# Score visits across batch borders, one mask on GpSimd and an earlier weight load in an attention + squared-ReLU kernel

## The chip, the cores and the metric

The kernel runs on one core of one Trainium2 chip. The metric is the device time of one execution in microseconds (us). Ratios are the mean time of one kernel's fast runs over that of the other kernel's fast runs of the same rounds, so they are not quite the ratio of the medians quoted beside them. The rounds of the experiments ran on three chips of the same kind, each with before measured in the same rounds, so ratios compare better than medians of different rounds.

## The reference

Attention with 16 "beacon" keys per head in front of the causal keys, then a feed-forward layer with squared ReLU, over all tokens. Cut to what matters:

```python
B, H, S, Nb, D = 8, 8, 576, 16, 64           # q, k, v: (B, H, S, D); beacon_k, beacon_v: (B, H, Nb, D)
scores = q @ concat(beacon_k, k).T / sqrt(D)  # causal for k, open for the 16 beacon keys
a = softmax(scores)
x = (a @ concat(beacon_v, v)) as (B*S, H*D)   # 4608 x 512
h = relu(x @ w_in)                            # w_in 512 x 2048
out = (h * h) @ w_out                         # w_out 2048 x 512
```

## The kernel before

The kernel is a list of small operations, each with a priority, dependencies and a guessed duration. A list scheduler in Python walks them once and so fixes the order of instructions on each engine; on the chip each engine then runs its own list in order and waits for semaphores. The order is thus a result of the guesses, but the times are the chip's. The attention of batches 1 to 7 is woven into the feed-forward work (first layer: `w_in`; second layer: `w_out`) of nine chunks of 512 tokens.

Three parts matter. First, the score matmuls of batches 1 to 7. A batch has 13 pieces of 512 columns (two heads each); TensorE does them in "visits" of two or three pieces, between other work:

```python
    PLAN = ((2,2,3,3,3),(2,2,3,3,3),(2,3,3,3,2),(2,3,3,3,2),(2,3,3,3,2),(2,3,3,3,2),(2,3,3,3,2))
    # ... in add_batch(b):
        for size in PLAN[b - 1]:
            pos = HP * b + 512.0 * n / PW
            runs = [(0,), (1, 2)] if size == 3 else [tuple(range(size))]
            # ... one PE op per run; a triple's first piece goes to two single PSUM banks, the rest to strips
            n += size
        assert n == NPC      # every batch ends with a visit of its own
```

Second, the triangle masks of batch 0 (a minimum with a triangle on VectorE; zeroing with an affine select on GpSimd), of which one is on GpSimd:

```python
        on_pool = n == 1 and p in (2, )
        mask = add(f"mask{p}.{n}", "POOL" if on_pool else "DVE", ...)
```

Third, the order of GpSimd's work in the start, where it issues nearly all loads and does some casts. `p1k` is a load of q or k, `v0` a load of v, `w0` a quarter of `w_in`, `c2` the cast of the third v load, `m2` the mask of pair 2:

```python
    SOFT = "t0 p1k p1q t1 p2k p2q v0 v1 p3k p3q v2 v3 v4 w0 w1 c2 c3 c4 w2 w3 m2".split()
    # then: batch 1's k and q, its v, and the four quarters of w_out
    w_ops["out", i] = add(f"wout{i}", "POOL", 1.3, emit, ..., dma=2.6)
```

The softmax here doesn't subtract the row's maximum and nothing guards it: scores larger than these inputs give would overflow.

## Time and profile before

| | before |
|---|---|
| time, median of the first three runs (and of 11 in later rounds) | 338.1 us (338.0) |
| span of the profiled execution | 336.9 us |
| TensorE matmul busy | 97% |
| VectorE, ScalarE, GpSimd busy | 51%, 56%, 28% |
| last quarter of w_out lands | 50.49 us |
| last matmuls of attention start (only feed-forward work after) | 263.3 us |

"Busy" is the share of the span with an instruction in flight. TensorE at 97% does not mean that it is at its peak: what can be read from the trace is when each matmul starts. The prediction below shows the lines.

### The profile page before, as it was taken

What the parts mean: (1) busy time and instruction counts of PE and PEld (TensorE: products, weight loads), DVE (VectorE), ACT (ScalarE), POOL (GpSimd) and SP (SyncE); (2) the same over time, 40 slices, a digit from 0 to 9 for tenths busy, and PEclk for the clock granted to TensorE, in tenths of its full rate; (3) what the DMA queues carried; (4) which work ended last, traced back from release to release, by engine and by line L of the source; (5) the groups of instructions that cost most, each with busy time, mean ns of one, the idle gap of its engine ahead of it and who ended that gap; (6) DMA issues with size and microseconds to landing.
All of it is one profiled execution on the core that took longest, in us unless ns stands there. A gap on an engine that the chain in (4) does not pass through costs nothing.

```text
span 336.9 us, 7807 instructions
## 1 busy us (share of the span) xinstructions
PE 328.4 (97%) x3153; PEld 188.0 (56%) x3196; DVE 170.6 (51%) x393; ACT 189.6 (56%) x287; POOL 93.3 (28%) x146
## 2 busy tenths in 40 slices
PE   8999999999999999999999999999999999999996
PEld 6587866444564554545458845554555544444444
DVE  4896986048646983477145723674247302301400
ACT  3875874277468735476647674666557216515621
POOL 9694714226305513250334142404000000000000
PEclk9999999999999999999999999999999999999999
DMA  7999999999999997999899999998210221011003
GB/s 138 216 193 217 205 182 205 230 243 214 173 230 221 193 199 141 222 235 186 150 213 215 166 196 163 219 229 159 74 62 2 46 90 62 0 61 66 1 2 125
DMA packets 143955, 51.74 MB, mean 154 GB/s; under 512 B 130702, under 2 KB 138798, under 8 KB 143918
## 3 DMA queue, kind: packets, MB, share of 16 engines
q1 hardware_dynamic: 135375, 42.19, 63.4%
q0 software_dynamic: 7904, 8.69, 15.3%
q8 instruction: 25, 0.41, 0.5%
q10 hardware_dynamic: 639, 0.36, 0.4%
q14 instruction: 12, 0.10, 0.1%
HBM read 37.22 MB, written 9.44 MB: 138 GB/s over the span
## 4 chain that ended last, share of the span: by engine, by line
PE 83%; DMA 10%; POOL 5%; issue 1%; ACT 0%; POOLq 0%; ACTq 0%
PE ps L955 35%; PE ps L917 33%; PE ps L754 8%; PE strip L624 4%; DMA w_out<-in_moe_w_out_dram 4%; DMA qk_area<-in_q_dram 3%; DMA stg<-in_v_dram 2%; PE ps L624 2%; POOL qk_area L452 2%; PE ps L867 1%; POOL stg L372 1%; PE ps L821 1%; POOL w_out L854 0%; POOL w_in L846 0%; POOL vb L328 0%
## 5 line engine op out<-in xcount | busy, mean ns | idle before, releaser
L917 PE MATMUL ps<-xT,w_in 128*128 128x512 bf16 (+3 forms) x686 | 131.4, 339 | 0.7
L955 PE MATMUL ps<-w_out,g 128*128 128x512 bf16 x535 | 127.1, 379 | 2.1 <-DMA w_out<-in_moe_w_out_dram 0.5
L917 PEld LDWEIGHTS <-w_in 128*128 128x128 bf16 x704 | 65.6, 98 | 51.0 <-issue 0.7
L933 ACT ACTIVATE g<-ps 128x512 bf16<-128x512 f32 (+2 forms) x113 | 64.0, 566 | 45.8 <-PE ps L917 42.7
L633 ACT ACTIVATE pt<-strip 128x1024 bf16<-128x1024 f32 (+3 forms) x86 | 81.2, 1003 | 13.1 <-PE strip L624 13.0
L942 DVE TENSOR_TENSOR g<-g 128x1024 bf16<-128x1024 bf16 (+2 forms) x80 | 51.1, 648 | 66.9 <-ACT g L933 65.4
L955 PEld LDWEIGHTS <-g 128*128 128x128 bf16 x560 | 51.5, 98 | 57.4 <-issue 2.1
L328 POOL CAST qk_area<-stg 128x512 bf16<-128x512 f32 (+2 forms) x60 | 40.9, 689 | 62.9 <-DMA stg<-in_k_dram 39.3
L326 ACT COPY osb<-ps 128x512 f32<-128x512 f32 (+2 forms) x32 | 18.1, 570 | 58.6 <-PE ps L955 48.8
L328 POOL CAST vb<-stg 128x512 bf16<-128x512 f32 (+1 forms) x38 | 25.2, 670 | 70.6 <-DMA stg<-in_v_dram 70.3
L754 PEld LDWEIGHTS <-pt 128*128 128x128 bf16 (+1 forms) x960 | 36.4, 98 | 11.8 <-issue 0.9
L754 PE MATMUL ps<-vb,pt 128*128 128x65 bf16 (+1 forms) x960 | 39.5, 194 | 0.1
L726 DVE TENSOR_TENSOR pt<-pt,tri 128x512 bf16<-128x512 bf16 x63 | 29.6, 478 | 17.6 <-ACT pt L675 10.9
L935 DVE TENSOR_SCALAR g<-ps 128x512 bf16<-128x512 f32 (+2 forms) x47 | 27.4, 598 | 13.1 <-PE ps L917 12.6
L773 DVE TENSOR_TENSOR xn<-ps,rcp 128x320 bf16<-128x320 f32 (+2 forms) x64 | 31.5, 492 | 2.5 <-DVE rcp L771 0.2
L675 ACT ACTIVATE pt<-ps 128x512 bf16<-128x512 f32 x42 | 22.8, 597 | 15.9 <-PE ps L624 13.3
L771 DVE RECIPROCAL rcp<-ps 128x5 f32<-128x5 f32 (+2 forms) x64 | 12.2, 190 | 32.1 <-PE ps L754 31.4
L624 PEld LDWEIGHTS <-kT 64*128 64x128 bf16 x596 | 19.8, 94 | 15.3 <-issue 13.6
L624 PE MATMUL strip<-qT,kT 64*128 64x208 bf16 (+13 forms) x474 | 27.0, 239 | 0.0
L328 DVE COPY osb<-ps 128x512 f32<-128x512 f32 (+1 forms) x6 | 3.8, 625 | 20.8 <-PE ps L867 11.7
L296 PE MATMUL ps<-g 128*128 128x128 bf16 (+1 forms) x82 | 9.7, 271 | 1.1 <-DVE warm L303 1.1
L372 POOL DMA_DIRECT2D stg<-in_v_dram x10 | 8.6, 875 | 4.0 <-DMA w_in<-in_moe_w_in_dram 2.8
(45 smaller groups left out, 98.4 us busy)
## 6 DMA issues: line engine op xcount, KB each, us to landing
out_dram<-osb SPq DMA_DIRECT2D x17, 512.0 KB, 4.4
stg<-in_q_dram SPq DMA_DIRECT2D x24, 256.0 KB, 4.8
stg<-in_k_dram SPq DMA_DIRECT2D x18, 256.0 KB, 5.3
stg<-in_v_dram SPq DMA_DIRECT2D x18, 256.0 KB, 4.9
w_in<-in_moe_w_in_dram POOLq DMA_DIRECT2D x4, 512.0 KB, 9.0
w_out<-in_moe_w_out_dram POOLq DMA_DIRECT2D x4, 512.0 KB, 11.5
stg<-in_v_dram POOLq DMA_DIRECT2D x6, 256.0 KB, 8.5
stg<-in_k_dram SPq DMA_DIRECT2D x6, 224.0 KB, 4.1
```

The lines of the kernel that those rows point to most:

```text
L328: eng[e].tensor_copy(dst, src)
L624: nc.tensor.matmul(st[hj][:, at:at + t1 - t0], kT[b % 2][hp, pr, 128 * c:128 * c + 128], qT[b % 2][hp, pr, t0:t1], start=True, stop=True,)
L633: nc.scalar.activation(pt[:, :, at:at + width], strips[qk.slots[s]][:, :, 0:width], AF.Exp, bias=0.0, scale=scale)
L675: nc.scalar.activation(pt[:, hj, at:at + 512], ps[qk.wide[hj]], AF.Exp, bias=0.0, scale=scale)
L726: nc.vector.tensor_tensor(out=d, in0=d, in1=tri[:, m0:m0 + m, :][:, None].to_broadcast([128, 2, m, 128]), op=ALU.min)
L754: nc.tensor.matmul(a[:, at + (t - tl[0]) * (D + 1):at + (t - tl[0] + 1) * (D + 1)], P[0:rr, hj, o:o + 128], vb[b % 2][0:rr, c, 2 * pr + hj ...
L773: nc.vector.tensor_tensor(out=xn[b % 2].rearrange("p t (h d) -> p h t d", d=D)[:, h0:h0 + nh, tl[0]:tl[0] + nt], in0=a[:, :, :, 0:D], in1= ...
L917: nc.tensor.matmul(h[:, lo - spans[0][0]:hi - spans[0][0]], w_in_sb[:, mc, ft * 128:(ft + 1) * 128], xT[:, mc, lo % RING:lo % RING + hi - lo],
L933: nc.scalar.activation(dst, h, AF.Relu, bias=0.0, scale=1.0)
L935: nc.vector.tensor_scalar(out=dst, in0=h, scalar1=0.0, scalar2=None, op0=ALU.max)
L942: nc.vector.tensor_tensor(out=d, in0=d, in1=d, op=ALU.mult)
L955: nc.tensor.matmul(o, G[:, fc, ts * 128:(ts + 1) * 128], w_out_sb[:, fc, :], start=(fc == 0), stop=(fc == NFT - 1))
```

## The change

The intent: fewer, fuller score visits from batch 4 on, less work for VectorE in the crowded start, and the third quarter of `w_in` in the queue before GpSimd sits down to wait for v. Cut to its core (the score code is reorganised into a class so that a visit can hold pieces of two batches; its instructions are the same):

```diff
-    PLAN = ((2,2,3,3,3),(2,2,3,3,3),(2,3,3,3,2),(2,3,3,3,2),(2,3,3,3,2),(2,3,3,3,2),(2,3,3,3,2))
+    sizes = list((2,2,3,3,3, 2,2,3,3,3, 2,3,3,3,2, 3,3,3,3,3,3,3,3,3,3,3,3,3,3,3,3,2,2))
...
+        for n in range(NPC):
+            if not opened:
+                opened.append(Visit(b, n, sizes.pop(0)))
+            opened[0].add(b, n)
+            if len(opened[0].parts) == opened[0].size:
+                opened.clear()
...
-        on_pool = n == 1 and p in (2, )
+        on_pool = n == 1 and p in (1, 2, )
...
-    (transposes of batch 0's first part: prio ... - 500.0; their copies to xT on DVE only)
+    (the same: prio ... - 2500.0; their copies on ACT or DVE)
...
-    SOFT = "t0 p1k p1q t1 p2k p2q v0 v1 p3k p3q v2 v3 v4 w0 w1 c2 c3 c4 w2 w3 m2".split()
+    SOFT = "t0 p1k p1q t1 p2k p2q v0 v1 p3k p3q v2 v3 v4 w0 w1 w2 c2 c3 m1 c4 w3 m2".split()
```

More of the change, by code (lines that the diff above doesn't have):

```diff
@@ L639, with __init__, emit, banks @@
     SHIFT = 0.25
-    PLAN = ((2,2,3,3,3),(2,2,3,3,3),(2,3,3,3,2),(2,3,3,3,2),(2,3,3,3,2),(2,3,3,3,2),(2,3,3,3,2))
     FREE = 2
-    last_qk = []
+    sizes = list((2,2,3,3,3, 2,2,3,3,3, 2,3,3,3,2, 3,3,3,3,3,3,3,3,3,3,3,3,3,3,3,3,2,2))
+    assert sum(sizes) == NPC * (B - 1)
+    last_qk, opened = [], []
+    class Visit:
+        def __init__(self, b, n, size):
+            pos = HP * b + 512.0 * n / PW
+            self.size, self.parts, self.ops = size, [], []
+            for k, run in enumerate([(0,), (1, 2)] if size == 3 else [tuple(range(size))]):
+                def emit(e, run=run):
+                    for s in run:
+                        bb, m = self.parts[s]
+                        emit_scores(bb, PIECES[m], self.banks(s))
+                self.ops.append(add(
+                    f"qk{b}.{n + run[0]}", "PE", (0.1 if size == 3 else 0.2) + 512 * len(run) / 2400.0, emit,
+                    prio=-1.0e6 if k else 100.0 * pos - 1000.0,
+                    behind=self.ops[-1:] if k else last_qk[-1:] if size == 3 or b > FREE else [],
+                    take=None if k else ("strip", "strip", min(size, 2)), gate=None if k else gate_at(pos - SHIFT)))
+            self.ops[0].wide = [None] if size == 3 else []
+            last_qk.append(self.ops[-1])
+        def banks(self, s):
+            first = self.ops[0]
+            if self.size == 3 and s == 0:
+                return [ps[x] for x in first.wide]
+            st = strips[first.slots[s - (self.size == 3)]]
+            return [st[:, 0, :], st[:, 1, :]]
+        def add(self, b, n):
+            s = len(self.parts)
+            self.parts.append((b, n))
+            first, op = self.ops[0], self.ops[-1 if s else 0]
+            at, prio = 512 * n, 1.0e-2 * (HP * b + 512.0 * n / PW) - 30.0
+            if self.size == 3 and s == 0:
+                es = []
+                for hj in range(2):
+                    def emit_half(e, hj=hj):
+                        nc.scalar.activation(pt[:, hj, at:at + 512], ps[first.wide[hj]], AF.Exp, bias=0.0, scale=scale)
+                    es.append(add(f"exp{b}.{n}.{hj}", "ACT", 0.18 + 512 / 1200.0, emit_half, prio=prio + 1.0e-4 * hj,
+                                  deps=[op], give=(first, hj - 2)))
+            else:
+                es = [add_exp(f"exp{b}.{n}", first, s - (self.size == 3), at, 512, prio, op)]
+            for pr in sorted({mm[0] for mm in PIECES[n]}):
+                p = HP * b + pr
+                for o in deps_of(b, pr, 0) + av_ops[p - HP]:
+                    if o not in first.need:
+                        first.need.append(o)
+                qk_ops[p].append(op)
+                exps_of[p] += es
@@ L647, in add_batch @@
             qk_ops[p], av_ops[p], exps_of[p] = [], [], []
-        n = 0
-        for size in PLAN[b - 1]:
-            pos = HP * b + 512.0 * n / PW
-            box = {}
-            runs = [(0,), (1, 2)] if size == 3 else [tuple(range(size))]
-            for k, run in enumerate(runs):
-                def emit(e, run=run, n=n, box=box, size=size):
-                    for s in run:
-                        if size == 3 and s == 0:
-                            emit_scores(b, PIECES[n], [ps[x] for x in box["qk"].wide])
-                        else:
-                            st = strips[box["qk"].slots[s - (size == 3)]]
-                            emit_scores(b, PIECES[n + s], [st[:, 0, :], st[:, 1, :]])
-                qk = add(f"qk{b}.{n + run[0]}", "PE", 0.2 / len(runs) + 512 * len(run) / 2400.0, emit,
-                         prio=-1.0e6 if k else 100.0 * pos - 1000.0, behind=[qk] if k else last_qk[-1:] if size == 3 or b > FREE else [],
-                         take=None if k else ("strip", "strip", min(size, 2)), gate=None if k else gate_at(pos - SHIFT))
-                last_qk.append(qk)
-                if k == 0:
-                    qk.wide = [None] if size == 3 else []
-                    box["qk"] = qk
-                for s in run:
-                    at, prio = 512 * (n + s), 1.0e-2 * (pos + 0.1 * s) - 30.0
-                    if size == 3 and s == 0:
-                        es = []
-                        for hj in range(2):
-                            def emit_half(e, hj=hj, at=at, qk=qk):
-                                nc.scalar.activation(pt[:, hj, at:at + 512], ps[qk.wide[hj]], AF.Exp, bias=0.0, scale=scale)
-                            es.append(add(f"exp{b}.{n}.{hj}", "ACT", 0.18 + 512 / 1200.0, emit_half, prio=prio + 1.0e-4 * hj, deps=[qk],
-                                          give=(qk, hj - 2)))
-                    else:
-                        es = [add_exp(f"exp{b}.{n + s}", box["qk"], s - (size == 3), at, 512, prio, qk)]
-                    for pr in sorted({mm[0] for mm in PIECES[n + s]}):
-                        p = HP * b + pr
-                        for o in deps_of(b, pr, 0) + av_ops[p - HP]:
-                            if o not in box["qk"].need:
-                                box["qk"].need.append(o)
-                        qk_ops[p].append(qk)
-                        exps_of[p] += es
-            n += size
@@ L689, in add_batch @@
-        assert n == NPC
+        for n in range(NPC):
[4 more added lines that the diff above has]
+                opened.clear()
         for pr in range(HP):
@@ L822, in emit_tp @@
                                             xn[b % 2][0:n, t, 128 * pr:128 * pr + 128], ident[0:n, 0:n])
-                tp = add(f"xtp{b}.{k}.{pr}", "PE", 0.02 + 0.05 * len(ph.tiles) + (0.1 if b == 0 else 0.0), emit_tp, prio=-120.0 - (500.0 if b == 0 and len(ph.tiles) == 2 else 0.0),
+                tp = add(f"xtp{b}.{k}.{pr}", "PE", 0.02 + 0.05 * len(ph.tiles) + (0.1 if b == 0 else 0.0), emit_tp, prio=-120.0 - (2500.0 if b == 0 and len(ph.tiles) == 2 else 0.0),
                          deps=norm_ops[HP * b + pr, k], take=("ps", "tp"))
@@ L831, in emit_ev @@
                     copy_on(e, xT[:, pr, at + lo:at + hi], pp[:, lo:hi])
-                o = add(f"xte{b}.{k}.{pr}", ("ACT", "DVE") if b or k else ("DVE",),
-                        {"ACT": 0.2 + (hi - lo) / 1200.0, "DVE": 0.12 + (hi - lo) / 960.0}, emit_ev, prio=-110.0 - (500.0 if b == 0 and len(ph.tiles) == 2 else 0.0),
+                o = add(f"xte{b}.{k}.{pr}", ("ACT", "DVE"),
+                        {"ACT": 0.2 + (hi - lo) / 1200.0, "DVE": 0.12 + (hi - lo) / 960.0}, emit_ev, prio=-110.0 - (2500.0 if b == 0 and len(ph.tiles) == 2 else 0.0),
                         deps=[tp], give=tp)
```

## The prediction

> **What bounds the kernel now.** I read the page first, for the busy shares and the chain that ended last.
>
> ```profile
> PE 328.4 (97%) x3153; PEld 188.0 (56%) x3196; DVE 170.6 (51%) x393; ACT 189.6 (56%) x287; POOL 93.3 (28%) x146
> PE 83%; DMA 10%; POOL 5%; issue 1%; ACT 0%; POOLq 0%; ACTq 0%
> ```
>
> TensorE is occupied for 328.4 of 336.9 us, and no other engine for more than 56%. The chain has 83% on PE and 15% on DMA and POOL together, so there are two regimes: a start that loads set, and a long rest that PE sets. The chain in order of time shows where one ends.
>
> ```profile
> 23.28 11.17 DMA qk_area<-in_q_dram
> 34.45 0.28 issue
> 34.73 1.48 POOL w_out L854 x2
> 36.22 0.63 issue
> 36.84 13.64 DMA w_out<-in_moe_w_out_dram
> 50.49 0.04 issue
> 50.53 0.38 PE ps L955
> ```
>
> The last quarter of w_out lands at 50.49 us, and from there to the tail the chain is PE almost without a break. I call that landing the gate. The waits of PE between 5 and 52 us, and between 52 and 320 us, are the whole list here:
>
> ```profile
> PE ps L955 <- DMA w_out<-in_moe_w_out_dram: 0.5, 1, 0.5
> PE ps L487 <- ACT g L933: 0.5, 1, 0.5
> PE ps L487 <- DMA qk_area<-in_k_dram: 0.5, 2, 0.3
> ...
> PE ps L955 <- issue: 0.2, 1, 0.2
> ```
>
> The first three are of the start, the fourth is all that the rest has. So after the gate there is no wait to win; only less work on PE, or cheaper switches between kinds of work, can shorten that part. A wait removed before the gate is worth something only if the gate moves too. The timeline of PE around the gate:
>
> ```profile
> 46.36 1.03 PE L955 MATMUL ps<-w_out,g 128*128 128x512 bf16 x4
> 47.22 0.63 PE L754 MATMUL ps<-vb,pt 128*128 128x65 bf16 x15
> 47.87 1.02 PE L955 MATMUL ps<-w_out,g 128*128 128x512 bf16 x4
> 48.83 0.40 PE L624 MATMUL ps<-qT,kT 64*128 64x208 bf16 x6
> 49.06 0.61 PE L624 MATMUL strip<-qT,kT 64*128 64x272 bf16 x12
> 49.59 0.43 PE L821 MATMUL ps<-ident,xn 112*128 112x112 bf16 x5
> 50.53 1.02 PE L955 MATMUL ps<-w_out,g 128*128 128x512 bf16 x3 [0.50 <-DMA w_out<-in_moe_w_out_dram]
> ```
>
> The four second-layer groups of the first token tile each need one quarter of w_out. The third starts at 47.87, as its quarter lands (47.83); then one score visit and one set of transposes run, and the fourth waits until 50.53. Those transposes were through by about 49.9 (the next kind of work follows such a set after some 0.26 us elsewhere), so there are about 0.65 us of slack on PE before the gate.
>
> What the gate itself hangs on is the stream of loads. All big early loads go through one queue in a fixed order. The landings in the trace are: w_in quarters at 20.38, 23.43, 25.97 and 28.81, batch 1's k and q from 30.00 to 34.45, its v until 40.44, w_out quarters at 42.75, 45.28, 47.83 and 50.49. A quarter in mid-stream takes 2.54 us after the one before it; the second of w_in took 3.05. The windows show why it might:
>
> ```profile
> 20.00:21.50 1.50, 1.50 (x38) 1.15 (x35) 1.31 (x5) 1.30 (x2) 1.50 (x5) 1.00 1.06 136
> 22.00:26.00 4.00, 4.00 (x78) 3.74 (x75) 3.21 (x12) 1.68 (x5) 3.34 (x5) 1.00 1.24 205
> ```
>
> The last column is GB/s: 136 in the stretch 20.0 to 21.5, 205 just after. There is a dip of 1.5 x (205 - 136) / 205 = 0.5 us of stream. It lies just after the third quarter was issued (18.80, below), when only the second was left in the queue.
>
> ```profile
> 11.68 1.57 POOL L846 DMA_DIRECT2D w_in<-in_moe_w_in_dram  x2
> 15.97 0.61 POOL L328 CAST vb<-stg 128x512 bf16<-128x512 f32 x1 [2.71 <-DMA stg<-in_v_dram]
> 17.60 1.25 POOL L328 CAST vb<-stg 128x512 bf16<-128x512 f32 x2 [1.02 <-DMA stg<-in_v_dram]
> 18.80 1.50 POOL L846 DMA_DIRECT2D w_in<-in_moe_w_in_dram  x2
> ```
>
> **What the Trainium skill says.** "TensorEngine Tiling (Array Packing)", Key Properties: "Changing tiling mode (not just tile) drains the TensorE". The scores use 64-row tiles and everything around them full rows, so each visit pays two changes; the trace agrees, with 0.22 us a visit (below). "DMA: Bandwidth & Descriptors", Queues, rings and completion order: each pair of queue row and engine is a ring of its own, consumed in ring order. So an earlier issue in the same order brings nothing forward unless a ring had run empty. The landings, in issue order, agree; the dip is the only sign of an empty ring. "Perfetto Trace Analysis", Tensor Engine Instruction: matmul ends are estimated, not observed. Therefore I count PE work by starts: first-layer matmuls of 512 columns start 0.2155 us apart.
>
> **The change, part by part.** (1) Visits across borders. The set of matmuls is the same; batches 4 to 7 have 52 pieces, in 4 x 5 = 20 visits before and in 16 triples and 2 pairs, 18, after. The cost of a visit beyond its columns: the pair at 257.10 us follows a matmul that started at 256.786, and the next first-layer matmul starts at 257.646, so 257.646 - 256.786 - 0.2155 = 0.645 us for 2 x 512 columns, which at 2400 columns per us are 0.427: 0.22 us over. The triple at 248.40 gives about the same (0.88 against 0.64). Two fewer are 2 x 0.22 = **0.45 us** saved, all after the gate. ScalarE does the same exps (four more triples, each with one piece as two halves, 8 more instructions of which only the fixed part is extra), at 56% and off the path.
>
> (2) The mask of batch 0's second pair on GpSimd. It takes 0.42 + some 0.5 us from VectorE near 17.3 to 18.3 and, by the one there before (0.80 + 0.35), puts 1.15 us on GpSimd. In the new order it stands between the fourth and fifth v cast. The fifth cast then ends near 19.95 instead of 18.85, so the first 24-matmul probability group waits longer; the order puts a set of transposes, a 6-matmul group and a score piece ahead of it, and two more filler matmuls, so PE is busy until about then anyway. Following the groups by their durations, I have first-layer work start near 23.7 us instead of 22.8, with 3 more transposes done, and batch 1's first transposes come at 30.3 instead of 30.05. There the 0.5 us wait falls away. In sum PE reaches the second layer at most 0.4 us later for its own work. That fits into the slack before the gate. GpSimd issues batch 1's loads about 0.6 us later (21.9 against 21.28), still 8 us ahead of the first landing.
>
> (3) The third w_in quarter ahead of the casts: it can go at about 13.4 us (a semaphore that comes at 13.33) instead of 18.80. It stands in the same place of the stream. If the ring ran empty at 20 to 21.5, up to 0.5 us is won and every later landing moves; I put **0.4 us** on it, so the gate at 50.1.
>
> (4) What stands where around the gate. The instruction order shows that before, one score triple (18 matmuls) was done ahead of the fourth quarter; now it comes after it, and one 15-matmul probability group comes ahead in its place. A triple is 0.77 us from its start to the next kind (48.83 to 49.6), a probability group 0.46 (256.14 - 255.68). So the work after the gate grows by 0.77 - 0.46 = **0.3 us**. PE comes to the fourth quarter near 49.65, so the wait stays, near 0.5 us.
>
> Sum: -0.4 (gate) + 0.3 (work moved behind it) - 0.45 (visits) = -0.55 us. 338.1 - 0.55 = **337.5 us**.
>
> **Rivals.** (a) The dip is no empty ring, only an engine of the sixteen that lags; w_out then lands at 50.5 as before and the change is worth +0.3 - 0.45: 337.9. For it: the first two quarters together took 5.24 us from the last v load, 2.62 each, hardly more than the 2.54 of mid-stream. (b) GpSimd becomes the bound of the start: the chain already runs through its casts and issues from 17.6 to 23.3, and the mask adds 1.15 us there. If the landings followed issue, the gate would move by 0.6 and the time be 338.5. Against it: loads land 8 us after issue, in a full queue. (c) New stalls after the gate: a visit across a border needs the next batch's transposed q and k earlier and holds strips of two batches; the triples take two of the four PSUM banks. At 0.2 us in all stalls now, this can only cost. 339 at worst. (d) The start is PE's after all and better by the wait at 30.05 and the dip: 336.8.
>
> **Range and chances.** The main terms are each half a microsecond or less, and the three runs of before lie at 337.91, 338.10 and 339.42. (a) and (b) give the upper part, (d) the lower: 336.6 to 338.6. Two per cent is 6.8 us, more than all idle time of PE outside head and tail, so within 2% has 0.98, and either side 0.01.
>
> **What would show it.** Right: w_in's third quarter issued near 13.4; the dip gone and w_out's last landing near 50.1; the fourth second-layer group still waiting for it; 0.22 us less PE time per visit dropped, and no new wait after the gate. Wrong: the last landing at 50.5 or later (step 3), PE reaching it late with no wait (step 2, then the start is PE-bound), or waits of PE on strips or on batch 5 to 7's transposes (step 1).

## The result, and the profile after

The changed kernel took 337.69 us (median of 4 runs, 337.23 to 338.07), before in the same rounds 338.09 us; the ratio is 0.9979 with a 95% interval of 0.9956 to 1.0001. A second set of six runs gave 337.80 us and a ratio of 1.0001 (0.9983 to 1.0018). So it is the same within the noise: the medians are 0.4 and 0.2 us lower, and the tighter second interval leaves room for a gain of 0.6 us at most.

The page of the profile after, busy time and the chain that ended last by engine:

```profile
PE 331.3 (99%) x3198; PEld 189.0 (56%) x3198; DVE 169.7 (50%) x387; ACT 192.5 (57%) x295; POOL 91.7 (27%) x149
PE 87%; DVE 4%; DMA 4%; SPq 2%; issue 1%; ACT 1%; POOL 0%; DVEq 0%; POOLq 0%; ACTq 0%
```

DMA and POOL had 15% of the chain and have 4% now; VectorE has come in with 4%. PE's busy time went up by 2.9 us although it does the same matmuls and two fillers more: in this trace all matmul records are there (3198), in that of before some 43 are missing. Small idle gaps of PE in the trace of before are mostly such holes, and the sums of busy time of the two can't be compared.

The same two stretches as in the prediction, with GB/s last:

```profile
20.00:21.50 1.50, 1.50 (x38) 1.10 (x34) 1.29 (x5) 1.26 (x3) 1.50 (x4) 1.00 1.25 203
22.00:26.00 4.00, 4.00 (x89) 3.60 (x85) 2.82 (x9) 2.35 (x6) 4.00 (x6) 1.00 1.25 205
```

The dip is gone in this execution. The third `w_in` quarter is issued at 13.26 us and the last `w_out` quarter lands at 49.21 us instead of 50.49. PE around that time:

```profile
47.26 1.89 PE L968 MATMUL ps<-w_out,g 128*128 128x512 bf16 x8
48.98 0.61 PE L767 MATMUL ps<-vb,pt 128*128 128x65 bf16 x15
49.44 0.42 PE L834 MATMUL ps<-ident,xn 112*128 112x112 bf16 x5
49.70 1.89 PE L968 MATMUL ps<-w_out,g 128*128 128x512 bf16 x8
51.52 0.40 PE L624 MATMUL ps<-qT,kT 64*128 64x208 bf16 x6
51.75 0.60 PE L624 MATMUL strip<-qT,kT 64*128 64x272 bf16 x12
52.29 1.04 PE L968 MATMUL ps<-w_out,g 128*128 128x512 bf16 x4
```

There is no wait for w_out left. The x8 stretches hold groups of two token tiles, so which group needs which quarter can't be seen here; the instruction lists say it. Before, the 13th second-layer matmul waits for the last quarter; after the change it is the 21st, the one at 52.29. So the last quarter is needed 3.1 us after it has landed, and the score triple at 51.52 runs ahead of it as it did before. (In the prediction I took the group at 49.70 for it.)

What took its place. All waits of PE from 5 to 52 us in the changed kernel, and the timeline row of the first:

```profile
PE ps L930 <- DVE g L948: 0.5, 1, 0.5
PE ps L484 <- DVE qk_area L328: 0.2, 1, 0.2
...
42.39 1.91 PE L930 MATMUL ps<-xT,w_in 128*128 128x272 bf16 x16 [0.47 <-DVE g L948]
```

A first-layer group waits for VectorE to empty a PSUM bank (a bank of the memory that matmuls write). It looks like the cost of the new start, but the traces of the experiments don't bear that out: the wait is 0.46 us in again_after, but it is absent in start_only and gate_late_after, which have the new start, and 0.15 and 0.59 us in again_before and gate_late_before, which have the old one. What goes with the new order around the gate is a wait further on, of transposes of batch 1 for VectorE near 57 us (start_only, below): from 0.07 to 0.76 us are lost there in the four traces of the new start and in gate_hidden, and at most 0.07 at such sets in the traces with the old order. Late in the kernel, the chain of the changed kernel in order of time has this at 223 us:

```profile
223.04 4.96 DMA kT<-qk_area
228.00 0.05 issue
228.05 0.40 PE ps L624 x6
```

The score visit at 228.05 us starts as batch 7's transposed k lands. It is not that this k is needed earlier than before: in before the first visit that reads it starts at 227.29 us (226.77 in again_before). The transposition comes later: in before it was issued at 219.98 us and landed at 225.93, in again_before 218.53 and 224.38. Why it comes later is open.

**A ledger.** Up to the last transposes of batch 2 and up to the last probability group of batch 7, TensorE has by then done the same work in all versions (checked by counting matmuls; only the fillers differ by two), so these two starts can be compared between traces. After the second, 73.6 us of pure feed-forward work follow in both. Us from the span's start; "visits" are those between the two points.

| trace | last transposes of batch 2 | from there to the last probability group | span |
|---|---|---|---|
| before, first / second | 101.35 / 101.07 | 161.94 / 161.71, 24 visits | 336.9 / 336.4 |
| changed, first / second | 101.11 / 100.77 | 161.61 / 161.62, 22 visits | 336.4 / 336.0 |
| w2_only | 100.37 | 161.69, 24 visits | 335.7 |
| visits_only | 100.16 | 162.25, 22 visits | 336.1 |
| start_only | 100.62 | 161.89, 24 visits | 336.2 |
| w2_visits | 100.60 | 161.32, 22 visits | 335.6 |
| w2_visits_b7 | 101.24 | 161.59, 22 visits | 336.5 |
| gate_hidden | 99.59 | 161.68, 22 visits | 334.9 |

The first column is the noisy one: between two executions of the same kernel it moved by 0.3 us, and by 1.2 us among the traces that have the start of before. Its mean is 100.9 us for the start of before (before twice, visits_only) and 100.8 us for the changed one (changed twice, start_only). The second is steadier (0.01 to 0.23 us between two executions), and there the change gained only 0.1 to 0.3 us.

### The profile page after: what moved, and what is told of

It is laid out like the page before. It is cut to its first block, busy times and chain, and to the rows that moved or that the text cites. A ratio compares the mean times of both kernels' runs of the same rounds, so it can differ in the third digit from the quotient of the medians.

```text
span 336.4 us, 7860 instructions
## 1 busy us (share of the span) xinstructions
PE 331.3 (99%) x3198; PEld 189.0 (56%) x3198; DVE 169.7 (50%) x387; ACT 192.5 (57%) x295; POOL 91.7 (27%) x149
## 4 chain that ended last, share of the span: by engine, by line
PE 87%; DVE 4%; DMA 4%; SPq 2%; issue 1%; ACT 1%; POOL 0%; DVEq 0%; POOLq 0%; ACTq 0%
PE ps L968 35%; PE ps L930 31%; PE ps L767 8%; PE strip L624 5%; PE ps L624 2%; DMA kT<-qk_area 1%; PE ps L296 1%; SPq L407 1%; DMA osb<-in_k_dram 1%; DVE g L948 1%; DMA stg<-in_k_dram 1%; PE ps L834 1%; PE ps L487 1%; PE ps L880 1%; DVE g L955 1%
## 5 line engine op out<-in xcount | busy, mean ns | idle before, releaser
L930 PE MATMUL ps<-xT,w_in 128*128 128x512 bf16 (+3 forms) x704 | 133.5, 340 | 0.5 <-DVE g L948 0.5
L968 PE MATMUL ps<-w_out,g 128*128 128x512 bf16 x560 | 131.1, 379 | 0.0
L946 ACT ACTIVATE g<-ps 128x512 bf16<-128x512 f32 (+2 forms) x116 | 66.1, 570 | 45.3 <-PE ps L930 44.6
L955 DVE TENSOR_TENSOR g<-g 128x1024 bf16<-128x1024 bf16 (+2 forms) x80 | 52.9, 668 | 70.0 <-ACT g L946 68.5
L633 ACT ACTIVATE pt<-strip 128x1024 bf16<-128x1024 f32 (+3 forms) x82 | 77.5, 1003 | 5.7 <-PE strip L624 5.4
L328 POOL CAST vb<-stg 128x512 bf16<-128x512 f32 (+1 forms) x38 | 23.6, 630 | 68.8 <-DMA stg<-in_v_dram 56.5
L679 ACT ACTIVATE pt<-ps 128x512 bf16<-128x512 f32 x50 | 27.1, 597 | 16.8 <-PE ps L624 16.7
L948 DVE TENSOR_SCALAR g<-ps 128x512 bf16<-128x512 f32 (+2 forms) x44 | 24.7, 581 | 12.3 <-PE ps L930 11.6
L624 PE MATMUL strip<-qT,kT 64*128 64x112 bf16 (+13 forms) x452 | 25.7, 238 | 0.0
L326 ACT COPY xT<-ps 128x576 bf16<-128x576 bf16 (+2 forms) x10 | 5.3, 531 | 9.8 <-PE ps L834 9.8
```

The costliest lines, as they stand in the source:

```text
L328: eng[e].tensor_copy(dst, src)
L624: nc.tensor.matmul(st[hj][:, at:at + t1 - t0], kT[b % 2][hp, pr, 128 * c:128 * c + 128], qT[b % 2][hp, pr, t0:t1], start=True, stop=True,)
L633: nc.scalar.activation(pt[:, :, at:at + width], strips[qk.slots[s]][:, :, 0:width], AF.Exp, bias=0.0, scale=scale)
L679: nc.scalar.activation(pt[:, hj, at:at + 512], ps[first.wide[hj]], AF.Exp, bias=0.0, scale=scale)
L930: nc.tensor.matmul(h[:, lo - spans[0][0]:hi - spans[0][0]], w_in_sb[:, mc, ft * 128:(ft + 1) * 128], xT[:, mc, lo % RING:lo % RING + hi - lo],
L946: nc.scalar.activation(dst, h, AF.Relu, bias=0.0, scale=1.0)
```

## The experiments

My theory after the result: the visits save what I said but new waits take most of it back; the start gains at the gate and loses to VectorE; the earlier issue moves the loads. Rivals: the landings merely drift from run to run; a visit costs nothing beyond its columns; the start is still bound by w_out.

**again_before** and **again_after**: both kernels unchanged.

> The kernel before, unchanged, once more. It tells how far the loads of two executions of one program lie apart. In the first profile of before the fifth v load landed at 18.19 us and the first w_in quarter at 20.38; in the profile after they landed at 17.67 and 19.69, though nothing ahead of them was changed. Theory A (the ring runs empty because the third w_in quarter is issued late): the second quarter lands about 3.05 us after the first again, whatever the level, and the last w_out quarter near 50.0 to 50.5. Theory B (the landings only drift from run to run): that distance is nearer 2.55 in this run. Time: within 0.2% of before.

> The changed kernel, unchanged, once more, for a tighter time and a second trace. Theory A: the second w_in quarter lands 2.5 to 2.6 us after the first, the last w_out quarter near 49.2 to 49.8, TensorE comes to it at about 49.7 without a wait, and the 0.5 us wait for VectorE near 42.4 us is there again. Theory B: the distance varies. Time: 0.1 to 0.2% below before.

Measured: 338.11 us (ratio 1.0005, 0.9989 to 1.0021) and 337.80 us (1.0001). The landings in the traces, in us; "lag" is the second w_in quarter after the first:

| trace | third quarter issued | lag | last w_in lands | last w_out lands |
|---|---|---|---|---|
| before | 18.80 | 3.05 | 28.81 | 50.49 |
| again_before | 18.39 | 2.58 | 27.36 | 50.07 |
| visits_only | 17.69 | 3.33 | 27.52 | 49.29 |
| pairs | 18.36 | 3.64 | 28.79 | 50.05 |
| changed | 13.26 | 2.57 | 27.32 | 49.21 |
| again_after | 13.22 | 2.59 | 27.20 | 48.94 |
| w2_only | 13.84 | 2.57 | 27.45 | 49.46 |
| start_only | 13.56 | 3.27 | 27.87 | 49.51 |
| w2_visits | 13.23 | 2.75 | 27.23 | 49.70 |
| w2_visits_b7 | 13.12 | 3.25 | 28.01 | 50.07 |
| w2_visits2 | 13.63 | 2.96 | 28.12 | 49.44 |

Neither theory holds as it stood. With the late issue the lag is sometimes absent (2.58 in again_before), and with the early issue it is sometimes there (3.25, 3.27). So the empty ring isn't what makes it, or not alone. On the mean, the early kernels have their last w_out at 49.5 us (seven traces) and the late ones at 50.0 (four), the 0.5 us that I expected, but the traces of each kind spread over 0.5 to 0.7 us on either side. What the lag is stays open. The wait for VectorE near 42.3 us came again in again_after (0.46 us).

**w2_only**: before, with one word moved.

```diff
-    SOFT = "... v4 w0 w1 c2 c3 c4 w2 w3 m2".split()
+    SOFT = "... v4 w0 w1 w2 c2 c3 c4 w3 m2".split()
```

> Before, with only the third w_in quarter issued ahead of the v casts; the order of TensorE around the gate stays that of before. Theory A: the second quarter lands 2.55 us after the first instead of 3.05, all later loads 0.5 us earlier, so the last w_out quarter near 50.0 or 49.7 and the second layer's fourth group starts with it; as TensorE had about 0.65 us of slack there, the time falls by 0.5 us. Theory B: no fixed shift, time as before. Rival C (casts on GpSimd and the batch 1 loads come later because the issue stands before them): no gain or a loss of up to 0.3 us.

Measured: 337.92 us, ratio 0.9996 (0.9981 to 1.0011). The last w_out quarter landed at 49.46 and its group started at 49.51. The trace did as expected, 0.7 us shorter than again_before, but the five timed runs show only 0.2 us on the mean (337.78 against 337.99), within the noise. What rival C rests on isn't there: batch 1's first load was issued at 19.92 us, not later than in before (21.28 and 20.90). A gain of 0.5 us is not shown.

**visits_only**: before, with the changed kernel's score visits and nothing else.

> Before, with only the score visits of batches 4 to 7 running on across batch borders; the start is that of before. By step 1 of the prediction: two visits fewer save 0.45 us. By the trace of the changed kernel: from the last transposes of batch 2 (101 us) to the last probability group (263 us) 0.33 us less than before, of which the visits are 0.44 and 0.11 goes to other switches. Rival: nothing is saved, or new waits come.

Measured: 337.50 us, ratio 0.9986 (0.9968 to 1.0004), the ledger's second column 162.25 us, 0.5 more than again_before. Most of it is in one wait, here as a timeline row:

```profile
227.74 0.40 PE L624 MATMUL ps<-qT,kT 64*128 64x112 bf16 x6 [0.64 <-DMA kT<-qk_area]
```

Batch 7's transposed k landed at 227.69 us and the visit that crosses into batch 7 waited 0.64 us for it. (Against w2_visits, which has the same visits, 0.7 of 0.9 us more are lost here and 0.2 near 112 us.) Both halves of the expectation came true, the saving and a new wait, the second larger in this execution; the timed runs are on the mean 0.5 us faster than before (337.48 against 337.99), so the wait may be shorter in most of them, which no trace shows.

**pairs**: before, with more visits instead of fewer, to measure what one costs.

```diff
-    PLAN = ((2,2,3,3,3),(2,2,3,3,3),(2,3,3,3,2),(2,3,3,3,2),(2,3,3,3,2),(2,3,3,3,2),(2,3,3,3,2))
+    PLAN = ((2,2,3,3,3),(2,2,3,3,3)) + 5 * ((2,2,2,2,2,2,1),)
```

> Before, with the score visits of batches 3 to 7 cut into six pairs and one single piece per batch instead of three triples and two pairs: seven visits a batch instead of five, ten more in all, the same matmuls. By step 1 (0.22 us a visit; 0.235 from the traces since) 2.2 to 2.4 us slower. If a visit cost nothing beyond its columns: as before.

Measured: 340.15 us, ratio 1.0068 (1.0039 to 1.0096). 0.0068 of 338 us are 2.3 us for ten more visits, 0.23 us each. The trace agrees. One pair between two feed-forward stretches:

```profile
129.79 1.03 PE L955 MATMUL ps<-w_out,g 128*128 128x512 bf16 x4
130.75 0.62 PE L624 MATMUL strip<-qT,kT 64*128 64x96 bf16 x12
131.29 2.76 PE L955 MATMUL ps<-w_out,g 128*128 128x512 bf16 x12
```

The fourth matmul of the first row starts 3 x 0.2155 us after 129.79, so 0.86 us pass from its start to 131.29; its own 512 columns and the pair's 2 x 512 are 3 x 0.2155 = 0.65, and 0.21 us are left. It is 0.21 us for each of the 17 pairs of this trace that stand so between feed-forward matmuls, and 0.22 for triples. The price of a visit is shown.

**start_only**: the changed start with the visits of before.

> The changed start (mask of the second pair on GpSimd, third w_in quarter early, transposes' priority and engine), with the score visits of before. If the start of the changed kernel gains at its gate and gives 0.3 us back behind it (a score triple moved there) and 0.3 more to a wait of a probability group between 55 and 58 us: TensorE at the fourth w_out group near 49.6 without a wait, from there to the end 286.7 to 286.9 us, time as before within 0.2 us. If the start is what makes the change faster: 0.3 to 0.5 us below before.

Measured: 338.02 us, ratio 1.0003 (0.9988 to 1.0019). The start of the change is worth nothing by itself that the interval (0.4 us down, 0.6 up) would show. Its parts were not separated: the second mask on GpSimd and the transposes' priority and engine were never run alone. The wait behind the gate was there, as a timeline row:

```profile
57.19 0.43 PE L821 MATMUL ps<-ident,xn 112*128 112x112 bf16 x5 [0.60 <-DVE xn L773]
```

Transposes of batch 1 wait for their normalisation. VectorE runs its list in order, and ahead of that normalisation (ended 57.13 us) it has masks from 54.27 to 56.50 us. The changed kernel has the same at 57.69 us, with 0.3 us lost between its stretch of second-layer matmuls and that set (0.1 in again_after and in gate_late_after, 0.25 in gate_hidden). That the masks come late because the score visit does in the new order is my reading; no run tested it. (The expectation took the group near 49.6 for that of the last w_out quarter; it is the one at 51.33, landed at 49.51. Its 286.7 us to the end is therefore of the wrong group.)

**gate_late_before** and **gate_late_after**: one more load of the size of a w_out quarter, ahead of the last one, into a buffer that is written again before it is read.

```diff
+                more = [] if i < 3 else [nc.gpsimd.dma_start(
+                    out=osb[1] (as 4 x 512 bf16), in_=moe_w_out.rearrange("(c p) f -> p c f", p=128)[:, 0:n, :])]
-                return [nc.gpsimd.dma_start(
+                return more + [nc.gpsimd.dma_start(
```

> Before, with one more load of a w_out quarter's size (into a buffer that is free at that time and written again later) ahead of the last quarter of w_out: the gate 2.5 us later, nothing else moved. In before the gate and TensorE's arrival lie within 0.3 us or so of each other, so 2.0 to 2.5 us slower. If the start were bound by TensorE's own work by far: less than 1.5.

> The same load in the changed kernel. There the last quarter lands 0.5 to 0.6 us before TensorE comes to it (48.94 to 49.21 against 49.55 to 49.70), so the same delay costs 1.9 to 2.0 us over the changed kernel: it waits at the gate and starts the fourth group near 51.6. If it were still bound by the landing: 2.5.

Measured: 342.99 us for before with the late gate (ratio 1.0155, 1.0121 to 1.0189, so 5.2 us), and 337.82 us for the changed kernel with it (0.9998, 0.9974 to 1.0023, so at most 0.8 us over before), against the changed kernel's 337.69 and 337.80. Both expectations were wrong in size. The last quarter landed at 53.10 us, 2.6 to 3.0 us later than in the traces of before, and at 52.59 us, 3.4 to 3.7 us later than in those of the changed kernel. The two rows where PE takes it up, first before, then changed:

```profile
53.14 1.02 PE L957 MATMUL ps<-w_out,g 128*128 128x512 bf16 x4 [2.41 <-DMA w_out<-in_moe_w_out_dram]
```

```profile
52.63 1.02 PE L970 MATMUL ps<-w_out,g 128*128 128x512 bf16 x4 [1.31 <-DMA w_out<-in_moe_w_out_dram]
```

In the changed kernel 52.6 us is where that group starts anyway (52.14 and 52.29 in its two traces), so the delay is hidden but for 0.3 to 0.5 us. (This execution had come there 0.9 us earlier, hence the wait of 1.31.) The order of the new start has moved the need for the last quarter some 2 us later; that is what took the DMA out of the chain. In before, the delay costs more than itself. The windows of gate_late_before, the granted clock third from the end:

```profile
53.00:54.00 1.00, 0.86 (x5) 0.38 (x4) 0.00 (x0) 0.00 (x0) 0.00 (x0) 1.00 1.03 234
54.00:55.00 1.00, 1.00 (x21) 1.00 (x20) 0.69 (x1) 0.00 (x0) 0.81 (x2) 0.55 0.87 197
55.00:56.00 1.00, 1.00 (x16) 0.72 (x14) 0.80 (x3) 0.00 (x0) 0.72 (x2) 0.50 0.81 179
56.00:57.00 1.00, 1.00 (x4) 0.43 (x3) 0.91 (x3) 0.00 (x0) 0.31 (x1) 0.50 1.03 230
57.00:58.00 1.00, 1.00 (x18) 0.69 (x16) 0.96 (x2) 0.00 (x0) 0.66 (x1) 0.74 1.00 228
```

After a wait of 2.41 us, TensorE ran at half its clock from about 54 to 57.5 us, which is some 1.7 us lost again. With the 2.6 to 3.0 us of later landing that makes 4.3 to 4.7 us; the span grew by 4.0 to 4.5 (340.9 against 336.9 and 336.4). The mean clock was 0.995 in all four runs, so it was not this execution alone. After the wait of 1.31 us in gate_late_after the clock stayed at 1.00. The Trainium skill describes such a gate ("TensorE: Matmul & The Clock Gate", What's actually happening: the default state is throttled, half the clock after an idle window of about 3.4 us, the full clock after about as much of sustained work). The half clock agrees, and so does its length of 3.4 us or so; that a wait of 2.41 us, less than such a window, was enough is this trace's.

**w2_visits**, **w2_visits_b7**, **w2_visits2**: towards a better version. The first is w2_only with the new visits; the second keeps visits from holding pieces of both batch 6 and batch 7; the third runs on across all borders from batch 2.

```diff
 w2_visits_b7
-    sizes = list((2,2,3,3,3, 2,2,3,3,3, 2,3,3,3,2, 3,3,3,3,3,3,3,3,3,3,3,3,3,3,3,3,2,2))
+    sizes = list((2,2,3,3,3, 2,2,3,3,3, 2,3,3,3,2, 3,3,3,3,3,3,3,3,3,3,3,3,3, 2,3,3,3,2))
 w2_visits2
+    sizes = [2,2,3,3,3] + 26 * [3]
```

> The start of before with only the third w_in quarter early, and the visits across borders: the two parts that gained, without the mask on GpSimd and the moved triple. Theory: fourth w_out group near 49.4, then 286.3 - 0.1 to 0.4 us to the end; 0.3 to 0.7 us below before, at or below the changed kernel. Rival: the wait for batch 7's transposed k near 227 us, 0.64 us in visits_only, is there again and takes the gain.

> As w2_visits, but batch 7 starts a visit of its own (no visit holds pieces of batches 6 and 7); the visits stay two fewer than before. If the crossing into batch 7 makes the wait for its transposed k, the wait near 227 us is gone and 0.6 us is won over w2_visits where that has it. Rival: the wait comes from the late transposition alone and stays.

> As w2_visits, but the visits run on across borders from batch 2 on, all triples: four visits fewer than before instead of two. By the price of a visit (0.235 us) 0.45 us below w2_visits, if no new wait comes. Rival: crossings need the next batch's q and k earlier and wait for them, and nothing is won.

Measured: 337.37 us (0.9987, 0.9972 to 1.0002), 337.20 us (0.9983, 0.9967 to 0.9999), and 341.10 us (1.0099, 1.0081 to 1.0118). In w2_visits, batch 7's k landed at 224.64 us and its visit started at 227.24 without a wait; so the wait comes from the late transposition and not from the crossing alone, and nothing could be won by keeping batch 7 apart: the 0.2 us between the two medians is noise. (gate_late_after, with the visits of the changed kernel, had the k at 226.31 us and its visit at 228.06 without a wait too.) In w2_visits the ledger's second column is 161.32 us, 0.4 less than again_before: with no new wait the two visits are worth their 0.46 us nearly whole. In w2_visits2 new waits came at once; all waits of PE from 52 to 320 us:

```profile
PE ps L767 <- DVE pt L739: 1.6, 1, 1.6
PE ps L930 <- DMA xT<-xn: 1.2, 1, 1.2
PE ps L834 <- DVE xn L786: 0.8, 1, 0.8
PE ps L968 <- issue: 0.3, 2, 0.2
```

A probability group waited for its mask (101.66 us), a first-layer group for transposed tokens, and a transposition for the normalisation. Four visits fewer would save 0.9 us at 0.23 each; the first three waits cost 3.6 us.

**gate_hidden**: w2_visits with the scheduler told that TensorE sees w_out later, so that it orders the groups around the last quarter as the changed kernel has them.

```diff
-    w_ops["out", i] = add(f"wout{i}", "POOL", 1.3, emit, ..., dma=2.6)
+    w_ops["out", i] = add(f"wout{i}", "POOL", 1.3, emit, ..., dma=2.6, late=1.5)
```

> As w2_visits, with one line more: the scheduler is told that TensorE sees each w_out quarter 1.5 us later, so it orders a second-token group and the rest around the last quarter as the changed kernel has them, without the mask on GpSimd. What the gate still costs in w2_visits (0.25 us of waiting in its trace, 0.55 in w2_visits_b7) goes; the last quarter is needed near 51.3 and landed before 50. Against it: in start_only and the changed kernel that order met a wait of transposes for VectorE near 57 us (0.6 and 0.4 us). Theory: the last transposes of batch 2 at 100.3 to 100.7 us, time within 0.2 us of w2_visits; if the order itself is what is worth having: 0.3 to 0.5 us below w2_visits.

Measured: 336.78 us (336.56 to 337.29), ratio 0.9953 (0.9934 to 0.9972) to before: 0.0047 of 338 us, so 1.6 us faster than before, and its median is 0.9 to 1.0 us below those of the changed kernel (337.69 and 337.80, in other rounds). It beats before clearly; of the changed kernel's two intervals its own lies clear of the second (0.9983 to 1.0018) and overlaps the first a little. The last quarter landed at 49.57 us and was taken up at 50.82 without a wait. All waits of PE from 5 to 320 us:

```profile
PE ps L968 <- issue: 0.5, 3, 0.2
PE ps L624 <- DMA kT<-qk_area: 0.3, 1, 0.3
PE ps L834 <- DVE xn L786: 0.2, 1, 0.2
```

The ledger places the gain in the start: the first column is 99.59 us against 101.07 and 101.35 in before, while the second, 161.68, is that of before, because in this trace the visit for batch 7's k lost 0.3 us (the second line). The gain over w2_visits, 0.6 us of the medians (1.1 by the ratios, whose intervals just touch), is more than the 0.25 us that its trace waited at the gate. A part may be that no execution's late landing reaches the end any more; in this trace TensorE also came to the second layer 0.8 us earlier (43.99 against 44.80) by the same order of work, which the edit does not explain; visits_only, with the start of before, came there at 44.00 too. That part stays open.

## Why the prediction was right or wrong

The time (337.5 predicted, 337.69 measured) and "within 2%" were right. That the sum came out is luck in part: its gain at the gate (0.4) and its loss behind it (0.3) all but cancel, neither came about as described, and the start as a whole measured nothing.

- **Where the bounds lie** held: loads to about 50 us, then TensorE. gate_late_before shows the first (a landing 2.6 to 3.0 us later costs more than that), pairs the second.
- **Step 1, the visits.** "0.22 us a visit" is shown by pairs (0.23 from the times, 0.21 from the trace; with the trace's own 0.2155 us for 512 columns the prediction's sum gives 0.645 - 0.431 = 0.21). "Two fewer are 0.45 us saved" failed as a net sum. Rival (c), new stalls behind the gate, came true beside it, though not as it was argued: batch 7's k was not needed earlier, it came later. Against again_before the stretch with the visits gained 0.1 us in both traces of the changed kernel (161.71 to 161.61 and 161.62). Of the waits that took the rest, two are in both traces: 0.2 us at a probability group near 185 us (0.69 and 0.68 us to the next matmul instead of 0.45), where the chain goes through VectorE's mask, and 0.12 to 0.14 us at the visit that waits for batch 7's k near 227 us. w2_visits, which has the same visits without these two, gained 0.4.
- **Step 2, the mask on GpSimd.** First-layer work started at 23.51 and 23.35 us, near the 23.7 predicted. The rest is not shown. The wait of 0.5 us at 30.05 us is gone, but not because TensorE came later: it came at 29.56 us instead of the 30.3 predicted, and batch 1's k had landed at 28.79 instead of 30.00; again_before, with no mask moved, has its k at 28.86 and no such wait either. That TensorE reaches the second layer later can't be seen: less the probability group that now stands ahead (0.46), the four traces of the new start come there at 44.43 to 45.47 us, those of the start of before at 44.00 to 45.91. The fifth cast ended at 19.15 us and not 19.95, and batch 1's loads were issued at 21.07 and not 21.9, so rival (b) did not come true. The start as a whole gave nothing (start_only 1.0003).
- **Step 3, the load.** The quarter was issued at 13.26 us as predicted, and the mean landing of the last w_out quarter moved by 0.5 us against the 0.4 predicted, with a spread as large as itself. "If the ring ran empty" is not supported: the lag came with the early issue too. By rival (a) the dip is something else, and that much fits; its last landing at 50.5 did not come. (In the section that the prediction names, the ring order is stated for the queues on which SP and ACT issue. These loads are GpSimd's; that they keep their order is shown here by their landings, which follow the order of issue in every trace.)
- **Step 4, the work around the gate, is the step that failed.** It said that the score triple "now comes after" the fourth quarter and that "the wait stays, near 0.5 us". In fact two groups of the second token tile and one probability group came ahead of the fourth quarter and the triple stayed ahead; the quarter is needed at 52.29 us, no wait is left, and the start is bound by TensorE's own work and its waits for VectorE (rival d, without its gain). gate_late_after shows this: a landing 3.4 us later cost nothing that its interval shows. The 0.3 us booked here as a loss for the moved triple did not come about, as the triple did not move; what the order costs instead is the wait for VectorE near 57 us, 0.1 to 0.8 us by the trace.
- The error came from counting groups in a merged list. The fourth second-layer group in order was taken for the one that needs the fourth quarter; the semaphore waits in the instruction list (13th against 21st matmul) would have told.

## What to carry to other kernels

When a load gates a stretch of work, look first at what else could stand ahead of the first use of that load: reordering hid some 3 us of delay here, while moving the load forward won at most 0.5. Count the price of a switch between kinds of work and test it by adding switches (ten more made 2.3 us plain, two fewer drowned in noise); then check in the trace what the merged work waits for, and look at more than one trace before a wait is put down to a change: the same program had a wait in one execution and not in the next. Where two terms are of the size of the run-to-run drift, compare traces at points of equal work done, not at the end.

## What the Trainium skill lacked or had wrong

- "TensorEngine Tiling (Array Packing)", Key Properties, says that a change of tiling mode drains TensorE but gives no price: here a visit of 64-row tiles between full-row matmuls cost 0.21 to 0.22 us for both changes in the traces (0.23 from the times of ten added visits).
- "TensorE: Matmul & The Clock Gate", What's actually happening, names an idle window of about 3.4 us: here a single wait of 2.41 us, between stretches of work, brought half the clock for about 3.4 us, and one of 1.31 us did not.
- "DMA: Bandwidth & Descriptors", Queues, rings and completion order, does not account for the lag seen here: the second of four equal loads in one queue landed 2.57 to 3.64 us after the first, changing between executions and kernels, with the next ones 2.50 to 2.84 us apart in most traces, whether the third had been issued 5 us earlier or not.
